# Chunk states summed by TensorE, the second group's units ahead of the weights, and low halves taken by a product with minus identity

## The chip, the cores and the metric

The kernel runs on one core of one Trainium2 chip. The metric is the device time of one execution in microseconds (us); the figure to beat is the median of several runs. Where a profile is shown, it is of one execution, and its engines are PE (TensorE matmuls), PEld (TensorE weight loads), DVE (VectorE), ACT (ScalarE), POOL (GpSimd) and SP (SyncE, which here only starts transfers).

## The reference

Two stages, in 32-bit floats. The first is gated linear attention with 4 batches, 8 heads, 768 positions and 48 values a head; the second is a feed-forward layer with GELU over all 3072 positions, 384 wide with 2048 hidden values. q, k, v and alpha come as 32-bit floats, the two weight matrices as 64-bit floats.

```python
for t in range(S):
    state = alpha[:, :, t, :, None] * state + einsum('bhd,bhe->bhde', k[:, :, t], v[:, :, t])
    y[:, :, t] = einsum('bhd,bhde->bhe', q[:, :, t], state)
x = y.transpose(0, 2, 1, 3).reshape(3072, 384)
h = x @ w_in
out = (0.5 * h * (1 + erf(h / sqrt(2)))) @ w_out
```

## The kernel before

**Attention.** The 3072 positions are 12 groups of 256 (three to a batch), and a group is handled in two units of four heads each, so there are 24 units. A unit's 256 positions are four chunks of 64. Running products of alpha along the positions, forward and backward, are DVE scans (`ahead`, lines 242 to 267); they scale q and k. On PE, `scores` (272) takes the products of k and q inside a chunk into a bank of PSUM, `turned` (285) transposes k there, ACT copies the transposed k out (`turned_out`, 294) and DVE masks the scores (`masked`, 299). `inside` (309) then writes one PSUM tile, `ybank`, that all units share: at line 319 the chunk's own part of the output, and at line 337 k times v for each chunk, which is what that chunk adds to the state. These are 64x64 products: the partitions hold chunk 0 or 2 in rows 0 to 63 and chunk 1 or 3 in rows 64 to 127, and two heads lie in the two halves of the output rows, so each product uses a quarter of the 128x128 array. A matmul with 32-bit floats shows as two PE instructions.

`chain` (346) adds these four contributions up on DVE, each onto the state before it, one instruction for each chunk (line 356, or a copy at 354 where a batch starts; the last chunk of a batch is left out). `outside_part` (369) multiplies q by the state ahead of its chunk into `ybank` (line 381), and waits for the last instruction of `chain`. `carry` (361) rescales the state for the next group.

**The split of x and of GELU.** The feed-forward products run in a shorter float format, fp32r, and each operand is kept as a high and a low half. ACT copies the finished `ybank` to the high half of x (`x_high`, 423); DVE subtracts that half from `ybank` to leave the low half (`x_low`, 427). `spread` (429) moves a strip of x between partitions by six transfers. For each group and each of eight slices f of 256 hidden values, `gemm1` (437) makes 18 matmuls (three products: high by high, low by high, high by low), ACT writes GELU twice (`gelus`, 455 and 456: rounded to the high half, and in full back into PSUM), DVE subtracts (`gelu_low`, 461) and `gemm2` (468) makes 12 matmuls into two accumulators that DVE empties when the group changes.

**The weights.** They arrive as 64-bit floats in 16 pieces, named a to p in turn from `w_in` and `w_out`; slice f needs pieces 2f and 2f+1. Each piece is turned into a high and a low half by ACT and DVE (`conversion`, 188): five DVE instructions, and a sixth at line 233 that leaves the low half. Three staging buffers hold pieces on the way.

**What sets the order.** The instruction order of PE, DVE, ACT and SP is written out ahead of time by a planner in the kernel (lines 585 to 821). It has a cost for each kind of step (`COST`), dependencies, and ranks; `ORDER` (31) gives the ranks of the first six units (digits) and of the pieces (letters). Each engine takes the ready step of lowest rank; PE fills the rest with `gemm1` and `gemm2`. The first three groups (`NSB`) run the feed-forward slices as pieces become ready; later groups follow when all pieces are converted. The order is then fixed: on the chip an engine waits at each instruction for what it needs. `pads` (99) fills unused rows of the operand tiles with 0 or 1 at the start.

Of the kernel before, what the change touches and what calls it, by code (L numbers as in the profile page):

```python
# [22 lines left out]
XB = 3  # L23
WAIT = 0.15
SLOW = 1.8
COST = dict(
    scan=2.25, back=2.05, q=1.35, scores=1.2, kn=0.6, mask=0.62, inside=1.2, chain=1.15, outer=0.85, carry=0.26,
    xh=0.6, xl=0.65, spread=2.0, check=0.95, load=2.6, fetch=0.4, u=0.92, c0=0.56, c1=0.9, c2=0.56, c3=0.95, c4=0.92,
    hi=0.84, lo=0.9, gemm1=2.12, gelu=0.58, low=0.63, gemm2=2.1, part=1.1,
)  # L30
ORDER = "0 1 a b c d 2 e 3 f g 4 h i 5 j k l m n o p"


@with_exitstack
def gla_then_gelu_ffn(ctx: ExitStack, tc: tile.TileContext, q, k, v, alpha, qg, kg, ag, w_in, w_out, out):
# [45 lines left out]
    def column(name, value):  # L81
        t = const.tile([P, 1], F32, name=name)
        nc.gpsimd.memset(t, value)
        return t

    zero, ones = column("zero", 0.0), column("ones", 1.0)
    lo_b, hi_b = column("lo_b", A_MIN), column("hi_b", -A_MAX)
    top = column("top", TOP).to_broadcast([P, G])
# [10 lines left out]
    def pads(i, n, p0, p1, eng):  # L99
        for r0 in (DP // 2, DP + DP // 2):  # L100
            r = slice(r0, r0 + DP // 2)
            t = data[i][n][r, p0:p1].rearrange("p a t -> p (a t)")
            if eng is nc.scalar:
                eng.copy(t, (ones if n == "a" else zero)[r].to_broadcast(t.shape))
            else:
                eng.memset(t, 1.0 if n == "a" else 0.0)

    for n in "akq":
        pads(0, n, 0, 1, nc.vector)
    for n, eng in (("a", nc.gpsimd), ("k", nc.scalar), ("q", nc.vector)):  # L110
        pads(0, n, 1, NPAIR, eng)
    for n, eng in (("a", nc.gpsimd), ("k", nc.scalar), ("q", nc.gpsimd)):
        pads(1, n, 0, NPAIR, eng)
    for t in vbuf:
        nc.gpsimd.memset(t[:, :, H * D :], 0.0)

    states = []
    for u in range(NU):
        states.append([const.tile([P, 2, D], F32, name=f"state{u}_{i}") for i in range(NCH + 1)])

    mask = const.tile([P, CS], F32, name="mask")
    nc.gpsimd.memset(mask, 1.0)
# [146 lines left out]
    def ends_batch(g, j):  # L269
        return g % GPB == GPB - 1 and j == NCH - 1  # L270
# [38 lines left out]
    def inside(g, u):  # L309
        d = cur[g, u]  # L310
        vn = vbuf[g % NB]
        for i in range(2):
            for j in range(NCH):
                c, b = j // 2, j % 2
                r, t = slice(b * CS, (b + 1) * CS), (2 * i + c) * CS
                for h in range(2):
                    o = slice(h * DP, (h + 1) * DP)
                    e = (4 * u + 2 * i + h) * D
                    nc.tensor.matmul(  # L319
                        ybank[o, b, t : t + CS],  # L320
                        lhsT=vn[r, c, e : e + DP],
                        rhs=d["ss"][r, h, 2 * i + c, :],
                        start=(i == 0 and c == 0),
                        stop=(j == 0 and g % GPB == 0),
                        skip_group_check=True,
                    )
        for j in range(NCH):
            if ends_batch(g, j):
                continue
            c, b = j // 2, j % 2  # L330
            r = slice(b * CS, (b + 1) * CS)
            for i in range(2):
                t = 2 * C + (2 * i + c) * D
                for h in range(2):
                    o = slice(h * DP, (h + 1) * DP)
                    e = (4 * u + 2 * i + h) * D
                    nc.tensor.matmul(  # L337
                        ybank[o, b, t : t + D],
                        lhsT=d["kn"][r, i, c * P + h * DP : c * P + (h + 1) * DP],
                        rhs=vn[r, c, e : e + D],  # L340
                        start=False,
                        stop=True,
                        skip_group_check=True,
                    )

    def chain(g, u):
        d = cur[g, u]
        st = states[u]
        for j in range(NCH):
            if ends_batch(g, j):  # L350
                continue
            new = ybank[:, j % 2, 2 * C : 2 * C + 4 * D].rearrange("p (i c d) -> p i c d", i=2, c=2)[:, :, j // 2]
            if g % GPB == 0 and j == 0:
                d["chain"] = nc.vector.tensor_copy(st[1], new)
            else:
                d["chain"] = nc.vector.tensor_tensor(out=st[j + 1], in0=new, in1=st[j], op=ALU.add)  # L356

    def carry(g, u):
        if ends_batch(g, NCH - 1):
# [65 lines left out]
    def x_low(g, u):  # L425
        for y, hi, lo in x_parts(g, u):
            nc.vector.tensor_tensor(out=lo, in0=y, in1=hi.bitcast(F32), op=ALU.subtract)

    def spread(g):
        x, z = cur[g, "x"], cur[g, "z"]  # L430
        for i in range(NK):
            for h in range(2):
                r0 = h * DP
                src = z[r0 + i * DR : r0 + (i + 1) * DR]
                eng = nc.scalar if h and g < NSB else nc.sync
                eng.dma_start(x[r0 + D : r0 + DP, i].bitcast(F32), src.bitcast(F32))

    def gemm1(g, f):
        xhi, xlo = xt[g]
        hp = ps_h.tile([P, 2, G], F32, tag="hp", name=f"hp_{g}_{f}")  # L440
        for j in range(2):
            for i in range(NK):
                for n, (a, x) in enumerate(((wi_hi[f], xhi), (wi_hi[f], xlo), (wi_lo[f], xhi))):
                    nc.tensor.matmul(  # L444
                        hp[:, j, :],
                        lhsT=a[:, j, i * P : (i + 1) * P],
                        rhs=x[:, i, :],
                        start=(i == 0 and n == 0),
                        stop=(i == NK - 1 and n == 2),
                    )  # L450
        return hp

# [6 lines left out]
    def gelu_low(g, f, hp, ghi):  # L459
        glo = ffn.tile([P, 2, G], F32R, tag="glo", name=f"glo_{g}_{f}")  # L460
        nc.vector.tensor_tensor(out=glo, in0=hp, in1=ghi.bitcast(F32), op=ALU.subtract)  # L461
        return glo

    parts = [const.tile([P, 2, DM], F32, name=f"part{i}") for i in range(NSB)]
    started = set()
# [144 lines left out]
    def op(*args, **kw):  # L610
        ops.append(Op(*args, **kw))
        return ops[-1]
# [4 lines left out]
    def plan_unit(n):  # L617
# [33 lines left out]
            free = [("x", g - XB - 1)]  # L651
        d["xh"] = op("ACT", "xh", lambda: (to_late(g, u), x_high(g, u)), [d["outer"]], rank=-1)
        d["free"] = free if u == 0 else []
        d["xl"] = op("DVE", "xl", lambda: x_low(g, u), [d["xh"]], rank=-0.5)
        if u == NU - 1:
            ready_x[g] = op("SP", "spread", lambda: spread(g), [d["xl"]], rank=-5, lands=2.2)
            if g >= NSB:
# [34 lines left out]
        return gemms.get((dep[1], NF2 - 1)) if next_f[dep[1]] == NF2 else False  # L692

    def when(o):
        d = next((v for v in unit.values() if v.get("xh") is o), None) if o.eng == "ACT" and o.cost == COST["xh"] else None
        at = o.at()
        if at is None or d is None:
            return at
        for dep in d["free"]:
            if isinstance(dep, tuple):  # L700
                dep = x_op(dep)
                if not dep:
                    return None
            if dep.end is None:
                return None
            at = max(at, dep.end + WAIT)
        return at
# [18 lines left out]
    def gemm1_op(g, t):  # L726
        f = next_f[g]
        next_f[g] += 1
        st = dict(g=g, f=f, first=g != state["g"], last=False)
        prev = steps[-1] if steps else None  # L730
        if st["first"]:
            if prev:
                prev["last"] = True
                prev["evac"] = Op("DVE", "part", lambda p=prev: p["out"](), [prev["gemm2"]], rank=-2)
                waiting["DVE"].append(prev["evac"])
            state["run"] += 1
        state["g"] = g
        two = steps[-2] if len(steps) > 1 else {}
        st["gemm1"] = Op("PE", "gemm1", lambda: st.update(hp=gemm1(g, f)))
        st["gelu"] = Op("ACT", "gelu", lambda: st.update(gh=gelus(g, f, st["hp"])), [st["gemm1"], two.get("gemm2")], rank=-3)  # L740
        st["gelu"].cost *= 2
        st["low"] = Op("DVE", "low", lambda: st.update(gl=gelu_low(g, f, st["hp"], st["gh"])), [st["gelu"], two.get("gemm2")], rank=-3)

        def second():
            if st["first"]:
                st["acc"] = [ps_o.tile([P, DM], F32, tag=f"acc{t}", name=f"acc{t}_{g}_{f}") for t in range(2)]
            else:
                st["acc"] = prev["acc"]
            st["out"] = gemm2(g, f, st["gh"], st["gl"], st["acc"], st["first"], st["last"], f == NF2 - 1)

        st["gemm2"] = Op("PE", "gemm2", second, [st["low"], prev and prev["gemm2"], prev and prev.get("evac")], rank=0)
        waiting["ACT"].append(st["gelu"])
        waiting["DVE"].append(st["low"])
        gemms[g, f] = st["gemm1"]
        steps.append(st)
        return st["gemm1"]
# [138 lines left out]
```

## Time and profile before

| | |
|---|---|
| median of 3 runs | 546.49 us (546.25 to 547.72) |
| the profiled execution | 546.99 us |
| its span, first to last instruction | 545.4 us |
| mean TensorE clock granted | 0.956 |
| PE busy | 508.4 us |
| DVE busy | 306.5 us |
| ACT busy | 201.3 us |
| POOL busy | 38.9 us |

Rows of groups give the line, the engine, the operation, what it writes and reads, the shape, the count, then busy time in us and the mean length of one in ns. Rows of time begin with the start in us from the span's start and the length in us. Lengths of matmuls overlap: the distance between starts is what one costs. In rows of stretches each engine's busy us and, in brackets, its instructions are given, then the clock that TensorE was granted as a share of full speed, the DMA share and GB/s.

### The profile page before, as it was taken

Reading aid. Unit: us, or ns where it says so; the run is one execution under the profiler, and the core shown is the slowest. Engines: PE = TensorE matmul, PEld = TensorE weight load, DVE = VectorE, ACT = ScalarE, POOL = GpSimd, SP = SyncE. Lnnn points to the kernel's source line nnn. Section 1 sums busy time; section 2 is a strip of 40 time slices with the busy share of each in tenths; the row PEclk is TensorE's granted clock in tenths of the full one; section 3 lists DMA queues with packets and bytes.
Section 4 is the critical chain, followed back from the end, with each engine's and each line's share of the span. In section 5 each row is a group of like instructions: output and inputs, shape, how many; then the busy total and the mean of one; then the engine's idle time right before and its main releaser. Section 6 shows DMA issues by size and latency. Waiting matters only on the chain.

```text
span 545.4 us, 13878 instructions
## 1 busy us (share of the span) xinstructions
PE 508.4 (93%) x5966; PEld 492.0 (90%) x5966; DVE 306.5 (56%) x573; ACT 201.3 (37%) x387; POOL 38.9 (7%) x51
## 2 busy tenths in 40 slices
PE   6547588999999999999999999999999999999996
PEld 6436588999999999999999999999999999999995
DVE  7999989999997878666337345142231221211211
ACT  3625345554443444433243243243223222222221
POOL 5000000000012121111001000000000000000000
PEclk9559589999999999999999999999999999999998
DMA  6974344533014344405005002001000000000001
GB/s 196 298 216 136 114 117 160 143 119 103 0 32 132 103 133 121 130 2 161 2 1 162 1 6 85 1 1 46 1 32 14 1 30 1 16 14 1 30 0 34
DMA packets 20723, 39.49 MB, mean 72 GB/s; under 512 B 4113, under 2 KB 7617, under 8 KB 20657
## 3 DMA queue, kind: packets, MB, share of 16 engines
q1 hardware_dynamic: 19136, 33.93, 20.7%
q0 software_dynamic: 1232, 4.33, 2.3%
q8 instruction: 49, 0.80, 0.6%
q10 hardware_dynamic: 288, 0.30, 0.2%
q14 instruction: 18, 0.14, 0.1%
HBM read 31.46 MB, written 4.72 MB: 66 GB/s over the span
## 4 chain that ended last, share of the span: by engine, by line
PE 84%; DVE 9%; DMA 2%; issue 2%; ACT 1%; ACTq 0%; DVEq 0%; SPq 0%
PE hp L444 37%; PE acc L472 35%; PE ybank L381 4%; PE s L290 2%; PE ybank L319 2%; PE s L281 2%; PE ybank L337 2%; DVE rp L262 1%; DVE st L217 1%; DVE pp L251 1%; DMA ad<-in_ag_dram 1%; DMA x<-z 1%; DVE w L202 1%; DVE state L356 1%; DVE w L227 1%
## 5 line engine op out<-in xcount | busy, mean ns | idle before, releaser
L444 PE MATMUL hp<-x,wih 128*128 128x256 f32 x1152 | 215.5, 287 | 7.6 <-DMA x<-z 7.6
L444 PEld LDWEIGHTS hp<-x,wih 128*128 128x128 f32 x1152 | 184.5, 193 | 8.9 <-ACT wih L230 7.8
L461 DVE TENSOR_TENSOR glo<-hp,ghi 128x512 fp32r<-128x512 f32 x96 | 66.1, 689 | 185.0 <-ACT hp L456 183.8
L444 PE MATMUL hp<-x,wil 128*128 128x256 f32 x576 | 163.9, 285 | 0.0
L455 ACT ACTIVATE ghi<-hp 128x512 fp32r<-128x512 f32 x96 | 57.5, 599 | 247.4 <-PE hp L444 247.3
L472 PE MATMUL acc<-woh,ghi 128*128 128x384 f32 x384 | 131.6, 343 | 1.4 <-ACT ghi L455 1.4
L472 PE MATMUL acc<-wol,ghi 128*128 128x384 f32 x384 | 128.6, 335 | 0.0
L444 PEld LDWEIGHTS hp<-x,wil 128*128 128x128 f32 x576 | 111.3, 193 | 0.0
L472 PE MATMUL acc<-woh,glo 128*128 128x384 f32 x384 | 82.2, 335 | 1.8 <-DVE glo L461 1.8
L472 PEld LDWEIGHTS acc<-woh,ghi 128*128 128x128 f32 x384 | 72.4, 188 | 2.6 <-ACT ghi L455 1.8
L472 PEld LDWEIGHTS acc<-wol,ghi 128*128 128x128 f32 x384 | 72.4, 189 | 0.0
L472 PEld LDWEIGHTS acc<-woh,glo 128*128 128x128 f32 x384 | 67.9, 188 | 2.2 <-DVE glo L461 2.2
L456 ACT ACTIVATE hp<-hp 128x512 f32<-128x512 f32 x96 | 57.1, 595 | 0.0
L258 POOL TENSOR_TENSOR qd<-qd,pp 128x512 f32<-128x512 f32 x18 | 23.2, 1287 | 226.0 <-DVE pe L252 158.3
L262 DVE TENSOR_TENSOR_SCAN rp<-ad,rp,top 128x255 f32<-128x255 f32 x48 | 35.3, 776 | 0.1
L381 PEld LDWEIGHTS ybank<-qd,state 48*48 48x48 f32 x704 | 23.7, 131 | 10.4 <-DVE state L356 6.6
L356 DVE TENSOR_TENSOR state<-ybank,state 128x96 f32<-128x96 f32 x80 | 20.5, 257 | 21.2 <-PE ybank L337 19.0
L381 PE MATMUL ybank<-qd,state 48*48 48x64 f32 x704 | 27.6, 233 | 5.3 <-DVE state L356 5.2
L251 DVE TENSOR_TENSOR_SCAN pp<-ad,top 128x256 f32<-128x256 f32 x48 | 30.4, 674 | 0.5 <-DMA ad<-in_ag_dram 0.5
L319 PEld LDWEIGHTS ybank<-ss,vn 64*64 64x64 f32 x768 | 14.5, 144 | 13.2 <-DVE ss L302 6.7
L319 PE MATMUL ybank<-ss,vn 64*64 64x64 f32 x768 | 18.0, 236 | 8.5 <-DVE ss L302 5.5
L496 POOL DMA_DIRECT2D out_dram<-part x11 | 8.3, 753 | 243.8 <-DVE part L490 164.6
(63 smaller groups left out, 397.0 us busy)
## 6 DMA issues: line engine op xcount, KB each, us to landing
st<-in_moe_w_in_dram SPq DMA_DIRECT2D x8, 768.0 KB, 4.8
st<-in_moe_w_out_dram SPq DMA_DIRECT2D x8, 768.0 KB, 4.8
ad<-in_ag_dram SPq DMA_DIRECT2D x48, 96.0 KB, 2.3
kd<-in_kg_dram SPq DMA_DIRECT2D x48, 96.0 KB, 2.3
qd<-in_qg_dram SPq DMA_DIRECT2D x48, 96.0 KB, 2.4
vn<-in_v_dram SPq DMA_DIRECT2D x12, 384.0 KB, 3.9
out_dram<-part POOLq DMA_DIRECT2D x11, 384.0 KB, 3.7
x<-z SPq DMA_DIRECT2D x63, 32.0 KB, 2.9
```

The source lines that it names most:

```text
L251: nc.vector.tensor_tensor_scan(pp[:, i], at[:, i], top, MID, ALU.mult, ALU.min)
L258: nc.gpsimd.tensor_tensor(out=qt, in0=qt, in1=pp, op=ALU.mult)
L262: nc.vector.tensor_tensor_scan(rp[:, i, G - 2 :: -1], at[:, i, G - 1 : 0 : -1], top[:, 1:], rp[:, i, G - 1 :], ALU.mult, ALU.min)
L281: nc.tensor.matmul(d["s"][o, h, e : e + CS], lhsT=d["kt"][r, i, t], rhs=d["qt"][r, i, t], start=True, stop=True)
L319: nc.tensor.matmul(ybank[o, b, t : t + CS], lhsT=vn[r, c, e : e + DP], rhs=d["ss"][r, h, 2 * i + c, :], start=(i == 0 and c == 0), stop=(j ...
L356: d["chain"] = nc.vector.tensor_tensor(out=st[j + 1], in0=new, in1=st[j], op=ALU.add)
L381: ins = nc.tensor.matmul(ybank[r, b, t : t + CS], lhsT=states[u][j][r, i], rhs=d["qt"][r, i, j * CS : (j + 1) * CS], start=False, stop=Tru ...
L444: nc.tensor.matmul(hp[:, j, :], lhsT=a[:, j, i * P : (i + 1) * P], rhs=x[:, i, :], start=(i == 0 and n == 0), stop=(i == NK - 1 and n == 2),)
L455: nc.scalar.activation(ghi, hp, AF.Gelu)
L456: nc.scalar.activation(hp, hp, AF.Gelu)
L461: nc.vector.tensor_tensor(out=glo, in0=hp, in1=ghi.bitcast(F32), op=ALU.subtract)
L472: nc.tensor.matmul(acc[t], lhsT=a[:, j, t * C : (t + 1) * C], rhs=w[:, j, :], start=(first and j == 0 and k == 0 and w is wo_hi[f]), stop= ...
```

## The change

Six edits.

1. **State sums in PSUM.** `inside` no longer writes each chunk's own contribution but the sum of all contributions up to and with the chunk: for chunks 2 and 3 the products of the first 128 positions and of the next are both accumulated. Where both chunks of a half are wanted, one product takes all 128 rows. `chain` is then one DVE instruction for a unit, which adds the carried state to all four sums (or copies them). The last chunk of a batch is no longer left out.
2. **Order.** The units of group 1 (2 and 3) go ahead of all weight pieces, and units 4 and 5 between pieces f and g.
3. **Low half of x, in the first three groups.** PE multiplies the high half by minus identity and accumulates into `ybank` (`x_minus`); ACT copies what is left (`x_rest`). DVE's subtraction goes.
4. **Low half of GELU, in the first three groups while the planner's clock is under 80 us.** The same: one matmul of 512 columns into the PSUM tile, and a copy by ACT (`gelu_rest`).
5. **One start flag for a tile in `gemm1`,** so that the later matmul accumulates on both halves.
6. **Pads.** DVE fills the pads of the first two pairs for all three tensors; the rest of q's goes to ACT. A minus identity is made by DVE at the start.

```diff
-    hi=0.84, lo=0.9, gemm1=2.12, gelu=0.58, low=0.63, gemm2=2.1, part=1.1,
+    hi=0.84, lo=0.9, gemm1=2.12, gelu=0.58, minus=0.35, low=0.63, gemm2=2.1, part=1.1,
-ORDER = "0 1 a b c d 2 e 3 f g 4 h i 5 j k l m n o p"
+ORDER = "0 1 2 3 a b c d e f 4 5 g h i j k l m n o p"
...
+    minus = const.tile([P, P], F32R, name="minus")
+    nc.vector.tensor_scalar(out=minus, in0=ident, scalar1=-1.0, scalar2=None, op0=ALU.mult)
...
     for n in "akq":
-        pads(0, n, 0, 1, nc.vector)
-    for n, eng in (("a", nc.gpsimd), ("k", nc.scalar), ("q", nc.vector)):
-        pads(0, n, 1, NPAIR, eng)
+        pads(0, n, 0, 2, nc.vector)
+    for n, eng in (("a", nc.gpsimd), ("k", nc.scalar), ("q", nc.scalar)):
+        pads(0, n, 2, NPAIR, eng)
...
         for j in range(NCH):
-            if ends_batch(g, j):
-                continue
-            c, b = j // 2, j % 2
-            r = slice(b * CS, (b + 1) * CS)
+            b = j % 2
             for i in range(2):
-                t = 2 * C + (2 * i + c) * D
+                t = 2 * C + (2 * (j // 2) + i) * D
                 for h in range(2):
                     o = slice(h * DP, (h + 1) * DP)
                     e = (4 * u + 2 * i + h) * D
-                    nc.tensor.matmul(
-                        ybank[o, b, t : t + D],
-                        lhsT=d["kn"][r, i, c * P + h * DP : c * P + (h + 1) * DP],
-                        rhs=vn[r, c, e : e + D],
...
+                    for c in range(j // 2 + 1):
+                        r = slice(0, P if c < j // 2 or b else CS)
+                        nc.tensor.matmul(
+                            ybank[o, b, t : t + D],
+                            lhsT=d["kn"][r, i, c * P + h * DP : c * P + (h + 1) * DP],
+                            rhs=vn[r, c, e : e + D],
...
     def chain(g, u):
         d = cur[g, u]
...
+        new = ybank[:, :, 2 * C : 2 * C + 4 * D].rearrange("p b (c e) -> p b c e", c=2)
+        to = held[u][:, 1:].rearrange("p (c b) e -> p b c e", b=2)
+        if g % GPB == 0:
+            d["chain"] = nc.vector.tensor_copy(to, new)
+        else:
+            old = held[u][:, 0].unsqueeze(1).unsqueeze(1).to_broadcast([P, 2, 2, 2 * D])
+            d["chain"] = nc.vector.tensor_tensor(out=to, in0=new, in1=old, op=ALU.add)
...
+    def x_minus(g, u):
+        for y, hi, _ in x_parts(g, u):
+            for b in range(2):
+                nc.tensor.matmul(
+                    y[:, :, :, b], lhsT=minus, rhs=hi[:, :, :, b], start=False, stop=True, skip_group_check=True
+                )
+
+    def x_rest(g, u):
+        for y, _, lo in x_parts(g, u):
+            nc.scalar.copy(lo, y)
...
+    def gelu_rest(g, f, hp, ghi):
+        nc.tensor.matmul(hp, lhsT=minus, rhs=ghi, start=False, stop=True, skip_group_check=True)
+
+        def out():
+            glo = ffn.tile([P, 2, G], F32R, tag="glo", name=f"glo_{g}_{f}")
+            nc.scalar.copy(glo, hp)
+            return glo
+
+        return out
...
-        d["xl"] = op("DVE", "xl", lambda: x_low(g, u), [d["xh"]], rank=-0.5)
+        if g < NSB:
+            d["xm"] = op("PE", "minus", lambda: x_minus(g, u), [d["xh"]], rank=-1)
+            d["xl"] = op("ACT", "xh", lambda: x_rest(g, u), [d["xm"]], rank=-1)
+        else:
+            d["xl"] = op("DVE", "xl", lambda: x_low(g, u), [d["xh"]], rank=-0.5)
...
+        if g < NSB and t < UNTIL:
+            st["minus"] = Op("PE", "minus", lambda: st.update(rest=gelu_rest(g, f, st["hp"], st["gh"])), [st["gelu"]], rank=-3)
+            st["low"] = Op("ACT", "gelu", lambda: st.update(gl=st["rest"]()), [st["minus"], two.get("gemm2")], rank=-2.9)
+            waiting["PE"].append(st["minus"])
```

In the planner `UNTIL` is 80.0 and the cost of `chain` goes from 1.15 to 0.5; that of `inside` stays at 1.2.

More of the change, by code (lines that the diff above doesn't have):

```diff
@@ L25 @@
 SLOW = 1.8
+UNTIL = 80.0
 COST = dict(
-    scan=2.25, back=2.05, q=1.35, scores=1.2, kn=0.6, mask=0.62, inside=1.2, chain=1.15, outer=0.85, carry=0.26,
+    scan=2.25, back=2.05, q=1.35, scores=1.2, kn=0.6, mask=0.62, inside=1.2, chain=0.5, outer=0.85, carry=0.26,
     xh=0.6, xl=0.65, spread=2.0, check=0.95, load=2.6, fetch=0.4, u=0.92, c0=0.56, c1=0.9, c2=0.56, c3=0.95, c4=0.92,
-    hi=0.84, lo=0.9, gemm1=2.12, gelu=0.58, low=0.63, gemm2=2.1, part=1.1,
+    hi=0.84, lo=0.9, gemm1=2.12, gelu=0.58, minus=0.35, low=0.63, gemm2=2.1, part=1.1,
 )
-ORDER = "0 1 a b c d 2 e 3 f g 4 h i 5 j k l m n o p"
+ORDER = "0 1 2 3 a b c d e f 4 5 g h i j k l m n o p"
 @with_exitstack
@@ L115, in gla_then_gelu_ffn @@
         nc.gpsimd.memset(t[:, :, H * D :], 0.0)
-    states = []
-    for u in range(NU):
-        states.append([const.tile([P, 2, D], F32, name=f"state{u}_{i}") for i in range(NCH + 1)])
+    held = [const.tile([P, NCH + 1, 2 * D], F32, name=f"state{u}") for u in range(NU)]
+    states = [[t[:, j].rearrange("p (i d) -> p i d", i=2) for j in range(NCH + 1)] for t in held]
     mask = const.tile([P, CS], F32, name="mask")
@@ L336, in inside @@
                     e = (4 * u + 2 * i + h) * D
-                    nc.tensor.matmul(
-                        ybank[o, b, t : t + D],
-                        lhsT=d["kn"][r, i, c * P + h * DP : c * P + (h + 1) * DP],
-                        rhs=vn[r, c, e : e + D],
[L341 to L344, printed above, removed]
+                    for c in range(j // 2 + 1):
[4 more added lines that the diff above has]
+                            rhs=vn[r, c, e : e + D],
+                            start=False,
+                            stop=True,
+                            skip_group_check=True,
+                        )
     def chain(g, u):
         d = cur[g, u]
[L348 to L356, printed above, removed]
+        new = ybank[:, :, 2 * C : 2 * C + 4 * D].rearrange("p b (c e) -> p b c e", c=2)
[5 more added lines that the diff above has]
+            d["chain"] = nc.vector.tensor_tensor(out=to, in0=new, in1=old, op=ALU.add)
     def carry(g, u):
@@ L427, in x_low @@
             nc.vector.tensor_tensor(out=lo, in0=y, in1=hi.bitcast(F32), op=ALU.subtract)
+    def x_minus(g, u):
[3 more added lines that the diff above has]
+                    y[:, :, :, b], lhsT=minus, rhs=hi[:, :, :, b], start=False, stop=True, skip_group_check=True
+                )
+    def x_rest(g, u):
+        for y, _, lo in x_parts(g, u):
+            nc.scalar.copy(lo, y)
     def spread(g):
@@ L447, in gemm1 @@
                         rhs=x[:, i, :],
-                        start=(i == 0 and n == 0),
+                        start=(j == 0 and i == 0 and n == 0),
                         stop=(i == NK - 1 and n == 2),
+                        skip_group_check=True,
                     )
@@ L694, in when @@
     def when(o):
-        d = next((v for v in unit.values() if v.get("xh") is o), None) if o.eng == "ACT" and o.cost == COST["xh"] else None
+        d = next((v for v in unit.values() if v.get("xh") is o), None) if o.name == "xh" else None
         at = o.at()
@@ L752, in gemm1_op @@
         waiting["ACT"].append(st["gelu"])
-        waiting["DVE"].append(st["low"])
+        waiting[st["low"].eng].append(st["low"])
         gemms[g, f] = st["gemm1"]
```

## The prediction

> **What bounds the kernel now.** I read the page first: the span and the slices.
>
> ```profile
> span 545.4 us, 13878 instructions
> ...
> PE   6547588999999999999999999999999999999996
> ```
>
> A digit is PE's busy share, in tenths, of a slice of 13.6 us. PE is full from the eighth slice to the end. So there are two stages, an opening of about 100 us and a long rest. The stretches give what each engine does in them.
>
> ```profile
> 50.00:100.00 50.00, 39.19 (x537) 35.62 (x536) 47.29 (x84) 22.98 (x43) 0.00 (x0) 0.83 0.41 128
> 54.10:71.20 17.10, 11.60 (x181) 10.59 (x182) 16.23 (x30) 5.00 (x10) 0.00 (x0) 0.50 0.44 123
> 100.00:400.00 300.00, 300.00 (x3932) 290.44 (x3931) 186.66 (x366) 119.19 (x243) 28.56 (x25) 1.00 0.23 68
> ```
>
> In the second half of the opening DVE is busy 47.29 us of 50 and PE 39.19: PE has gaps while DVE has next to none. From 100 us PE has no gap, at the full clock: what is added to PE there is added to the end, what is taken from DVE there is worth nothing. Between 50 and 100 us PE loses 50 - 39.19 = 10.8 us idle, and 11.60 us of work at half clock (54.1 to 71.2) would have taken half, another 5.8 us. That is 16.6 us. Before 50 us PE has gaps too, but until the first weights and the first x there is little to fill them with. So the change is a trade: less on DVE in the opening, against more on PE everywhere.
>
> **Part 1, the state sums: what PE pays.** The change removes three of four DVE adds and adds matmuls at line 337. Before, a unit has 4 chunks x 2 x 2 = 16 products, 32 PE instructions. After, chunks 2 and 3 have two products each, so 24 products, 48 instructions, and at the end of a batch, where there were 12, also 24. The shape changes too: 16 of the 24 use all 128 rows. What does one cost?
>
> ```profile
> 207.92 0.86 PE L472 MATMUL acc<-woh,glo 128*128 128x384 f32 x4
> 208.71 0.82 PE L381 MATMUL ybank<-qd,state 48*48 48x64 f32 x22
> 209.33 0.27 PE L281 MATMUL s<-qd,kd 48*64 48x64 f32 x2
> 209.36 0.23 PE L381 MATMUL ybank<-qd,state 48*48 48x64 f32 x2
> ...
> 213.18 0.68 PE L337 MATMUL ybank<-vn,kn 64*64 64x48 f32 x32
> 213.79 0.50 PE L444 MATMUL hp<-x,wih 128*128 128x256 f32 x2
> 214.13 0.28 PE L444 MATMUL hp<-x,wil 128*128 128x256 f32 x1
> 214.25 0.28 PE L444 MATMUL hp<-x,wih 128*128 128x256 f32 x1
> ```
>
> ```profile
> L337 PE MATMUL ybank<-vn,kn x704: 205/218/338, 16.7 to 402.9; 64*64 64x48 f32 x176
> ```
>
> One instruction of line 337 lasts 0.218 us, so the starts of the 32 spread over 0.68 - 0.22 = 0.46 us. They lie in four quarters of the array (two halves of rows, two of columns), so a quarter takes 8 of them in 0.46 us: 0.058 us each. Line 381 uses two quarters only: 22 instructions, 11 in each, over 0.82 - 0.22 = 0.60 us, that is 0.060 us over ten steps. So a quarter needs about 0.058 us for an instruction whether two or four quarters work, and they work on their own: line 281 begins in a free quarter at 209.33, ahead of the last of line 381 at 209.36.
>
> A product of 128 rows takes both row halves of its column half. Each column half has 12 products, 24 instructions, and all of them use the upper row half: 24 x 0.058 = 1.39 us in place of 0.46. That is 0.93 us more for a unit, and at the end of a batch, where there were six steps, 18 more instead of 16. No row shows a product of 128 rows by 64 columns, so the price is bounded from both sides. Below: line 444 moves 256 columns in 0.12 us (214.13 to 214.25), so 48 columns moved twice need 0.045 us by its rate, and the unit 24 x 0.045 = 1.08 us. Above: if PE must empty before it goes from one shape of product to another. That shows at the seams: four of line 472 at 0.17 us from 207.92 would have let line 381 begin at 208.61, it begins at 208.71; the last of line 337 begins at 213.64, and 0.058 later is 213.70, line 444 begins at 213.79 and its first two take 0.34 in place of 0.24. So a change of shape costs 0.10 to 0.19 us. In chunk 2 the change alternates between 128 and 64 rows: with the two changes around it that would be nine seams in a unit. I take 0.058 without seams, since it rests on rows of the same shape in columns and the quarters run independently.
>
> The TensorEngine Tiling (Array Packing) page of the Trainium skill, under Tiling Modes, Key Properties, says otherwise: "Changing tiling mode (not just tile) drains the TensorE", and it lists 128x64 and 64x64 as different configurations. By it the seams would be paid, and the sum would be that of the second rival. The trace agrees for 128x128 against quarters (the 0.10 to 0.19 us); it holds no case of the pair in question.
>
> In the full stage lie groups 3 to 11, 18 units, six at the end of a batch. Steps after: 18 x 24 = 432. Before: 12 x 8 + 6 x 6 = 132. Added: 300 x 0.058 = **+17.4 us**, with nothing to hide it.
>
> **Part 2, what DVE gains.**
>
> The groups of DVE, then one of ACT:
>
> ```profile
> L262 DVE TENSOR_TENSOR_SCAN rp<-ad,rp,top 128x255 f32<-128x255 f32 x48 | 35.3, 776 | 0.1
> L251 DVE TENSOR_TENSOR_SCAN pp<-ad,top 128x256 f32<-128x256 f32 x48 | 30.4, 674 | 0.5 <-DMA ad<-in_ag_dram 0.5
> L356 DVE TENSOR_TENSOR state<-ybank,state 128x96 f32<-128x96 f32 x80 | 20.5, 257 | 21.2 <-PE ybank L337 19.0
> ...
> L202 DVE SCALAR_TENSOR_TENSOR w<-st,u 128x768 int32<-128x768 int32 x16 | 15.3, 957 | 0.4
> ...
> L490 DVE COPY part<-acc 128x384 f32<-128x384 f32 x23 | 11.7, 550 | 2.5 <-PE acc L472 2.5
> L212 DVE TENSOR_SCALAR u<-w 128x768 int32<-128x768 int32 x16 | 8.9, 556 | 0.3
> ...
> L427 DVE TENSOR_TENSOR x<-ybank,x 128x512 fp32r<-128x512 f32 x12 | 8.2, 682 | 0.0
> ```
>
> ```profile
> L423 ACT CAST x<-ybank 128x512 fp32r<-128x512 f32 x12 | 7.1, 588 | 9.5 <-PE ybank L381 9.5
> ```
>
> For a unit: `chain` goes from four at 0.26 (1.03) to one of the size of the accumulator copy, 0.55; the subtraction for x, 0.68 or a little more in two parts, goes. That is 1.2 us for each of six units, 7 us. GELU's subtraction, of the shape of line 427's, goes at 0.68 for about six steps under the planner's 80 us, 4 us. So DVE has some 11 us less to do in the opening. ACT gets as many copies, 0.59 each, about 7 us on an engine that is busy for 23 of the 50 us to 100: hidden, unless a copy that waits for PE holds up the conversions queued behind it on ACT (their results feed DVE); I estimate under 2 us, in the range.
>
> PE pays too. A low half of x is 512 columns through minus identity, two times 0.12 by line 444, plus a change of shape, say 0.4 us a unit. A GELU step is 512 columns, 0.24 us.
>
> **Part 3, the order.** The first scan, and then the last step of the second piece of the first, third and fifth slice of the eight, which says when these weights are ready now:
>
> ```profile
> 5.53 1.27 DVE L251 TENSOR_TENSOR_SCAN pp<-ad,top 128x256 f32<-128x256 f32 x2 [0.52 <-DMA ad<-in_ag_dram]
> ...
> 27.69 0.95 DVE L233 TENSOR_TENSOR wol<-w,woh 128x768 fp32r<-128x768 f32 x1
> ...
> 65.48 0.95 DVE L233 TENSOR_TENSOR wol<-w,woh 128x768 fp32r<-128x768 f32 x1
> ...
> 102.99 0.95 DVE L233 TENSOR_TENSOR wol<-w,woh 128x768 fp32r<-128x768 f32 x1
> ```
>
> A unit costs DVE about 7.1 us now: two scans each way (2.9), two scalings and the mask of 128x512 at 0.68 (2.0), chain (1.0), low half (0.7) and small ones; after, 5.9. A piece has four instructions like line 202 and two like line 212, 4.9 us, so a slice 9.9. After, four units come first: the first scan at about 5.5 (it waits for its transfer) plus 4 x 5.9 is 29, then slices at about 39, 49 and 59, units 4 and 5 until 71, slices at 81 and 91. The first slice is 10 us later, the third 7 earlier, the fifth 13 earlier. The loads of units 2 and 3 are moved on SP's queue ahead of three fetches of weights; DVE has 29 us of units to do meanwhile, so a first piece that lands some 5 us later is still in time.
>
> What PE can do with it hangs on x. All units share `ybank`, so each must be finished before the next writes it.
>
> ```profile
> 15.80 1.13 PE L319 MATMUL ybank<-ss,vn 64*64 64x64 f32 x32 [4.14 <-DVE ss L302]
> 16.71 1.10 PE L337 MATMUL ybank<-vn,kn 64*64 64x48 f32 x32
> ...
> 24.33 1.13 PE L319 MATMUL ybank<-ss,vn 64*64 64x64 f32 x32 [2.92 <-DVE x L427]
> ...
> 36.94 0.77 PE L444 MATMUL hp<-x,wih 128*128 128x256 f32 x2 [7.59 <-DMA x<-z]
> ```
>
> The period is 24.33 - 15.80 = 8.5 us now. After, line 337 takes 16 more steps of about 0.1 at half clock (1.10 - 0.30 over eight), +1.7; the shorter chain gives back 0.5; a matmul and a copy in place of a subtraction add 0.6: about 10 us. Unit 0 at 15, so unit 3 ends near 55, its copies with it, and with the transfer x of group 1 arrives near 59 (now 7.59 us pass from the last product of unit 1 to the first `gemm1`, copies and transfer together). The first `gemm1` stays near 37 to 39 (x now, weights after). At 50 us PE stands about where it does now: one slice of group 0 through, half a step less of the second, one unit's share more. From 59 on there is work for two groups: three slices each, 17 us, with units 4 and 5 some 10 us more, then slices at 81 and 91 for three groups. So PE should be full from about 59 us, in place of about 95. Of the 16.6 us lost now after 50 us I leave 7: half of 50 to 59 with its slow clock, and some gaps at the units. **Gain 10 us.** Bounds: 0 if group 1 comes as late as before, 21 if nothing is lost after 50 us and unit 3's PE work (about 4.5 us) is done by then.
>
> PE's added work in the opening that is not hidden, after 59 us: two and a half units at 0.93 and two more batch-end steps each in units 4 and 5 (2.6), the low halves of x for three units (1.0), five GELU products (1.2): **+4.8 us**. Minus identity, pads and start flag: the memsets move between engines by 0.2 to 0.5 us ahead of a first scan that waits for its transfer; nothing.
>
> **The sum,** against the profiled execution's 546.99 us (545.4 plus 1.6 around it): + 17.4 - 10 + 4.8 = 559.2; the median lies 0.5 lower, so **558.7 us**.
>
> **The rivals.** *Cheap products, faster.* If a product of 128 rows costs only its stream, 0.045 us, the full stage gains 432 x 0.045 - 132 x 0.058 = 11.8 us and the opening 3.7; with the opening's gain between 10 and 21 us that is 541 to 552, and faster from a gain of 15.5 us on. For it: `ybank` is finished sooner as well. Against it: 48 and 64 columns cost the same 0.058 to 0.060 in the rows, so the stream isn't what sets it. 0.22. *Seams.* If each change of shape inside line 337 empties PE: nine times 0.10 to 0.19, and chunk 2's sixteen instructions run one after another in place of in pairs (+0.46), so 1.4 to 2.2 us a unit over 20.5 units, 28 to 45 us: 587 to 603, about 595. For it: the seams that the rows show. Against it: no row shows one between products with equal columns. 0.20. *No gain in the opening.* PE's longer units at half clock hold `ybank`, group 1's x comes as late as now, and the gain is 0: 568.7. 0.10. That edit 4 does little because few steps fall under the planner's 80 us would move the sum by 1 us and is in the range.
>
> **How the numbers follow.** The forecast has 0.48, with its own range 549 to 568. About 0.3%, or 1.6 us, is what a measurement can tell from no change. Faster: 0.13 from the cheap products and 0.02 from the forecast's edge, 0.15. Same: 0.04 and 0.03, 0.07. Slower: the rest, 0.78. The range leaves out the best 0.08 of the cheap products and half of the seams, about 0.11: 543 to 594.
>
> **What would show it.** Line 337: 1152 instructions instead of 704, and in the full stage 1.4 us from its first start to the next line's (1.1 with cheap products, 3 with seams). Line 356 gone, one instruction of 128x384 near 0.55. PE without gaps from about 60 us, the half-clock stretch of 54 to 71 us gone. The slices of PE full at the end as before. I am wrong if line 337 costs under 1 us a unit, or if PE is full well before 50 us.

## The result

The changed kernel takes 595.73 us (593.87 to 597.41) against 546.85: 8.9% more, ratio 1.0892 (1.0855 to 1.0928). The range of the prediction ended at 594. The direction, and that TensorE pays for the state sums, came as forecast; the size is that of the second rival, the seams.

The page after, in part: the shares of the engines, the slices of PE, the chain that ended last, and the groups of the state sums on PE and DVE.

```profile
span 594.4 us, 14762 instructions
...
PE 576.1 (97%) x6437; PEld 548.3 (92%) x6437; DVE 298.7 (50%) x494; ACT 206.6 (35%) x403; POOL 38.5 (6%) x51
...
PE   6998998999999999999999999999999999999996
...
PE hp L454 35%; PE acc L493 34%; PE ybank L338 13%; PE ybank L380 4%; PE ybank L321 3%; PE s L292 2%; PE s L283 2%; DVE rp L264 0%; ACT hp L467 0%; PE hp L476 0%; ACTq L446 0%; DVE pp L253 0%; ACT ghi L466 0%; ACT x L437 0%; PE ybank L431 0%
...
L338 PE MATMUL ybank<-vn,kn 128*64 128x48 f32 (+1 forms) x1152 | 82.6, 239 | 0.0
...
L355 DVE TENSOR_TENSOR state<-ybank,state 128x384 f32<-128x384 f32 x16 | 8.9, 557 | 54.4 <-PE ybank L338 54.4
```

PE was 508.4 us busy, now 576.1. The state sums (line 338 now, 337 before) were 2% of the chain and are 13%. DVE's `chain` is one instruction of 0.557 us, as forecast, and waits 54.4 us for those products.

A unit of the full stage after, and then one at the end of a batch before (the prediction shows a usual one before, at 213.18):

```profile
100.23 0.69 PE L321 MATMUL ybank<-ss,vn 64*64 64x64 f32 x32
100.75 3.20 PE L338 MATMUL ybank<-vn,kn 64*64 64x48 f32 x48
103.88 0.39 PE L454 MATMUL hp<-x,wih 128*128 128x256 f32 x1
```

```profile
97.97 0.62 PE L337 MATMUL ybank<-vn,kn 64*64 64x48 f32 x24
98.52 0.45 PE L472 MATMUL acc<-woh,ghi 128*128 128x384 f32 x1
```

From the first start of the sums to the next line's start: 103.88 - 100.75 = 3.13 us, where 1.39 was forecast and 0.61 (0.55 at the end of a batch) stood before. All 18 units of the full stage take 3.13: 18 x 3.13 - 12 x 0.61 - 6 x 0.55 = 45.7 us of the 48.9 measured. The other 3.2 us, uncertain by some 2 us as the interval of the ratio is, were lost in the opening. Inside the unit, in stretches cut at chunks 0, 1, 2 and 3, with the instructions of this line alone (those still running from the stretch before are counted again):

```profile
100.74:101.05 0.31, 0.30 (x8) 0.27 (x8) 1.00 0.00 0
101.05:101.33 0.28, 0.28 (x12) 0.27 (x9) 1.00 0.00 0
101.33:103.24 1.91, 1.91 (x22) 1.48 (x18) 1.00 0.19 26
103.24:103.88 0.64, 0.64 (x18) 0.58 (x16) 1.00 0.61 115
```

Chunks 2 and 3 have 16 instructions each. Chunk 3's are all of 128 rows and take 0.64 us with the way out to the next line; chunk 2's alternate between 128 and 64 rows and take 1.91, that is 0.24 for each of eight products.

The second half of the opening and the full stage, in the same stretches as before:

```profile
50.00:100.00 50.00, 45.98 (x621) 41.57 (x620) 43.02 (x64) 26.62 (x52) 1.29 (x1) 0.96 0.50 155
100.00:400.00 300.00, 300.00 (x3705) 284.72 (x3704) 177.36 (x296) 106.80 (x215) 26.37 (x23) 1.00 0.22 64
```

Between 50 and 100 us PE is busy 45.98 us (39.19 before), at a granted clock of 0.96 (0.83), and the half-clock stretch of 54 to 71 us is gone. That is not a gain yet, since the longer sums count as busy. The first half of the opening, before and then after:

```profile
0.00:50.00 50.00, 29.23 (x443) 26.86 (x444) 44.28 (x78) 23.06 (x36) 7.48 (x22) 0.73 0.69 210
0.00:50.00 50.00, 41.28 (x523) 36.47 (x524) 38.45 (x70) 22.27 (x40) 7.21 (x22) 0.63 0.63 190
```

Here the clock is lower than it was, 0.63 in place of 0.73, and at half clock the first unit's sums take 5.04 us to the next line's start where 0.83 stood before. The first `gemm1` begins late, at 48.01 in place of 36.94:

```profile
48.01 0.79 PE L454 MATMUL hp<-x,wih 128*128 128x256 f32 x2
```

What the feed-forward layer had done by 100 us, `gemm1` and `gemm2` before, then the same two after (busy us and count of PE, then of PEld):

```profile
0.00:100.00 100.00, 19.36 (x126) 18.60 (x126) 0.78 0.55 169
0.00:100.00 100.00, 15.93 (x80) 13.73 (x81) 0.78 0.55 169
...
0.00:100.00 100.00, 15.28 (x107) 14.53 (x108) 0.80 0.56 173
0.00:100.00 100.00, 12.86 (x60) 11.95 (x60) 0.80 0.56 173
```

The changed kernel is behind by 19 and 20 matmuls, with the sums of six units done in both. So the opening, which was to gain, lost a little. From 100 us PE is as busy as it was, 300 us of 300, with fewer instructions in them, 3705 for 3932: the waits inside the sums show as busy time.

### The profile page after: what moved, and what is told of

It reads as the page before. It is cut to its first block, busy times and chain, and to the rows that moved or that the text cites. A ratio compares the mean times of both kernels' runs of the same rounds, so it can differ in the third digit from the quotient of the medians.

```text
span 594.4 us, 14762 instructions
## 1 busy us (share of the span) xinstructions
PE 576.1 (97%) x6437; PEld 548.3 (92%) x6437; DVE 298.7 (50%) x494; ACT 206.6 (35%) x403; POOL 38.5 (6%) x51
## 4 chain that ended last, share of the span: by engine, by line
PE 94%; DVE 3%; ACT 1%; issue 1%; ACTq 0%; DVEq 0%
PE hp L454 35%; PE acc L493 34%; PE ybank L338 13%; PE ybank L380 4%; PE ybank L321 3%; PE s L292 2%; PE s L283 2%; DVE rp L264 0%; ACT hp L467 0%; PE hp L476 0%; ACTq L446 0%; DVE pp L253 0%; ACT ghi L466 0%; ACT x L437 0%; PE ybank L431 0%
## 5 line engine op out<-in xcount | busy, mean ns | idle before, releaser
L454 PE MATMUL hp<-x,wih 128*128 128x256 f32 x1152 | 213.3, 285 | 0.0
L472 DVE TENSOR_TENSOR glo<-hp,ghi 128x512 fp32r<-128x512 f32 x91 | 62.7, 689 | 184.7 <-ACT hp L467 184.6
L338 PE MATMUL ybank<-vn,kn 128*64 128x48 f32 (+1 forms) x1152 | 82.6, 239 | 0.0
L338 PEld LDWEIGHTS ybank<-vn,kn 128*64 128x64 f32 (+1 forms) x1152 | 68.3, 145 | 12.7
L299 ACT COPY kn<-s 128x512 f32<-128x512 f32 x24 | 14.1, 587 | 86.7 <-PE ybank L338 72.3
L264 DVE TENSOR_TENSOR_SCAN rp<-ad,rp,top 128x255 f32<-128x255 f32 x48 | 36.6, 803 | 0.1
L355 DVE TENSOR_TENSOR state<-ybank,state 128x384 f32<-128x384 f32 x16 | 8.9, 557 | 54.4 <-PE ybank L338 54.4
```

The source lines that it names most:

```text
L264: nc.vector.tensor_tensor_scan(rp[:, i, G - 2 :: -1], at[:, i, G - 1 : 0 : -1], top[:, 1:], rp[:, i, G - 1 :], ALU.mult, ALU.min)
L299: nc.scalar.copy(d["kn"], d["s"][:, :, 2 * C : 4 * C])
L338: nc.tensor.matmul(ybank[o, b, t : t + D], lhsT=d["kn"][r, i, c * P + h * DP : c * P + (h + 1) * DP], rhs=vn[r, c, e : e + D], start=False ...
L454: nc.tensor.matmul(hp[:, j, :], lhsT=a[:, j, i * P : (i + 1) * P], rhs=x[:, i, :], start=(j == 0 and i == 0 and n == 0), stop=(i == NK - 1 ...
```

## The experiments

The ratios are to the kernel before as timed beside each run (medians of 547.60 to 547.68 us).

**1. The same products, grouped by shape** (e1_grouped).

```diff
-        for j in range(NCH):
+        for j, c in ((0, 0), (2, 1), (1, 0), (2, 0), (3, 0), (3, 1)):
...
-                    for c in range(j // 2 + 1):
```

> The changed kernel with the same 24 products of the state sums in another order: first the eight of 64 rows, then the sixteen of 128 rows, so that nine changes of shape in a unit become one. Theory (each change of shape empties TensorE, 0.15 us): a unit's sums take 8 x 0.058 + 0.15 + 16 x 0.058 = 1.54 us in place of 3.13, 18 full-stage units give back 28.6 us, the opening a few more: 559 to 567. Rival (the products themselves or their number are dear, 48 instructions at 0.065 us): nothing changes, 594 to 597. Second rival (two products in a row that add to the same place in PSUM wait for each other): also about 563, since chunk 2's pairs are taken apart too; the next run tells it from the theory.

**2. The same order, chunk 2 all of 128 rows** (e2_rows128).

```diff
-                        r = slice(0, P if c < j // 2 or b else CS)
+                        r = slice(0, P if j else CS)
```

> The changed kernel in its own order, but chunk 2's second product takes 128 rows like its neighbours, so that chunk 3 is wrongly counted in chunk 2's sum: the same count, order and places in PSUM, only eight of nine changes of shape gone. Theory (change of shape): 0.23 + 0.15 + 20 x 0.058 = 1.54 us a unit, 559 to 567 in all. Rival (two products in a row into the same place wait): 3.1 us a unit, 594 to 597. Rival (number of products): 594 to 597.

**3. Five changes of shape in place of nine** (e8_five_seams): the alternating order for one `i` of chunk 2, and for the other both products of 64 rows first, then both of 128.

```diff
...
+        todo += [(2, 0, h, c) for h in range(2) for c in range(2)]
+        todo += [(2, 1, h, c) for c in (1, 0) for h in range(2)]
...
```

> The changed kernel with chunk 2's products taken apart by shape for one of two pairs of heads only: five changes of shape in a unit in place of nine, and half of the products that had to run alone. Theory: 28 x 0.058 + 5 x 0.15 = 2.37 us a unit, between 3.13 and 1.62, and 577 to 581 in all. Rival (one change of shape in the unit is enough to lose all, or only the last ones count): near 595 or near 562.

A unit of the full stage in each, in that order:

```profile
168.89 1.69 PE L337 MATMUL ybank<-vn,kn 64*64 64x48 f32 x48
170.51 0.39 PE L453 MATMUL hp<-x,wih 128*128 128x256 f32 x1
```

```profile
174.47 1.72 PE L338 MATMUL ybank<-vn,kn 64*64 64x48 f32 x48
176.12 0.39 PE L454 MATMUL hp<-x,wih 128*128 128x256 f32 x1
```

```profile
164.94 2.46 PE L340 MATMUL ybank<-vn,kn 64*64 64x48 f32 x48
167.33 0.44 PE L495 MATMUL acc<-woh,ghi 128*128 128x384 f32 x1
```

| kernel | changes of shape | a unit's sums, us | median, us | ratio to before |
|---|---|---|---|---|
| changed | 9 | 3.13 | 595.73 | 1.0892 (1.0855 to 1.0928) |
| five seams | 5 | 2.39 | 579.14 | 1.0577 (1.0538 to 1.0616) |
| rows 128 | 1 | 1.65 | 562.97 | 1.0278 (1.0231 to 1.0326) |
| grouped | 1 | 1.62 | 561.51 | 1.0271 (1.0229 to 1.0314) |

All have 48 instructions a unit. The number of products is not the cause, since it never changes. Two products in a row that add to the same place are not the cause either: experiment 2 keeps them at 1.65 us a unit, and chunk 3 of the changed kernel has them too. What changes is the shape, and the price follows the count: from one to five, 2.39 - 1.62 = 0.77 us, of which four products that run alone in place of in pairs take 4 x 0.058 = 0.23; the rest is 0.135 us for each change. From five to nine it is much the same: 0.74 less 0.23 is 0.51, 0.128 for each. The starts inside a unit of the changed kernel agree: the first instruction after a change starts 0.15 us after the one ahead of it, in place of 0.058, and its partner 0.094 after that, together 0.128 more. What TensorE does in that time no run shows; the profile models the ends of matmuls, so it can't show the array empty.

**4. The sums alone, and all but the sums** (e4_sums_only, e3_no_sums: the edits to `inside`, `chain` and the state tiles put into the kernel before, or taken out of the changed one, with the planner's cost of `chain`).

> The kernel before with the state sums alone. Theory: 46 us in the full stage and some 2.5 to 4 us for each of the last opening units: 595 to 605, about 599. Rival (the new order and the copies on ScalarE are a good part of the loss): 570 to 590.

> The changed kernel with the state sums undone: the chunks' own contributions and four adds on VectorE, as before; the order, the products with minus identity and the pads stay. Theory: the whole loss is the sums' (18 x 2.52 + 6 x 0.15 = 46 us in the full stage, and 2 to 20 us of the opening), and the other edits help: 528 to 541, about 535. Rival (the new order costs too, since the first weights come 19 us later): 547 to 552.

The sums alone: 601.24 us, ratio 1.0972 (1.0954 to 1.0990). All but the sums: 540.93, ratio 0.9876 (0.9854 to 0.9898), at the upper end of what was expected. So the sums are the whole loss, and the rest is a gain of 6.7 us; 53.6 lost and 6.7 gained leave 46.9, which is the measured 48.9 within the noise.

**5. Where the opening's gain comes from** (e6_order_only, the edit shown on the kernel before; e7_old_order, the run without the sums with this line as it was before).

```diff
-ORDER = "0 1 a b c d 2 e 3 f g 4 h i 5 j k l m n o p"
+ORDER = "0 1 2 3 a b c d e f 4 5 g h i j k l m n o p"
```

> The kernel before with the new order alone: group 1's units ahead of the weights, sums and low halves on VectorE as before. Theory (half of the opening's gain is that both groups share each slice): 542 to 546. Rival (only the relief of VectorE helps, and the later weights cost): 547 to 552.

> The run without the state sums, in the old order: the products with minus identity and the pads alone. Theory (half the gain is the relief of VectorE, some 8 us of subtractions): 542 to 545. Rival (the relief is worth its full length): 538 to 541; rival (copies on ScalarE and waits of TensorE eat it up): 546 to 549.

The order alone takes 548.88, ratio 1.0027 (1.0005 to 1.0048): a miss, no gain. The products with minus identity and the pads in the old order take 544.28, ratio 0.9932 (0.9909 to 0.9956), as expected. One reason why the order alone is worth nothing shows on ScalarE. The run with the order alone:

```profile
11.67 0.58 ACT L297 COPY kn<-s 128x512 f32<-128x512 f32 x1 [5.63 <-PE s L290]
...
22.00 0.89 ACT L194 ACTIVATE u<-st 128x768 f32<-128x768 f32 x1 [8.91 <-DMA st<-in_moe_w_in_dram]
...
23.50 0.57 ACT L297 COPY kn<-s 128x512 f32<-128x512 f32 x1
```

ScalarE stands 8.91 us before the scaling of the first weight piece, whose transfer now comes after those of units 2 and 3, and unit 1's copy of k is queued behind it until 23.50. In the run without the sums VectorE stands 4.0 us (3.89 with the order alone) before the mask that waits for that copy:

```profile
24.00 0.69 DVE L305 TENSOR_TENSOR ss<-s,mask 128x512 f32<-128x512 f32 x1 [4.03 <-ACT kn L300]
```

**6. That copy ahead of the scaling** (e5_copy_first on the run without the sums, e9_order_copy_first on the order alone).

```diff
         plan_unit(n)
+    wops[0]["u"].deps.append(unit[1]["kn"])
```

> The run without the state sums, with one dependency more in the planner: on ScalarE the copy of unit 1's transposed k goes ahead of the scaling of the first weight piece, which waits until 21.9 us for its transfer and holds that copy from about 18.7 to 23.4. Theory (the moved weight transfers hold up ScalarE, and behind it the units): unit 1 comes 4 us earlier, the idle 4.0 us of VectorE at 20 to 24 us goes, and 2 to 4 us of it reach the end: 537 to 539. Rival (the opening is bound by the weights on VectorE alone): no change, 540 to 542.

> The kernel before with the new order and, on ScalarE, unit 1's copy of the transposed k ahead of the scaling of the first weight piece. Theory (the new order itself helps, and the wait for the piece's transfer took that back): the 4 us at 20 to 24 us go and 544 to 546 is left, against 548.9 with the order alone. Rival (the order is worth nothing without the relief of VectorE): 547.5 to 550.

In the first of the two, ScalarE and then VectorE:

```profile
18.78 0.59 ACT L300 COPY kn<-s 128x512 f32<-128x512 f32 x1 [4.99 <-PE s L293]
22.01 0.92 ACT L197 ACTIVATE u<-st 128x768 f32<-128x768 f32 x1 [2.64 <-DMA st<-in_moe_w_in_dram]
```

```profile
19.93 0.68 DVE L305 TENSOR_TENSOR ss<-s,mask 128x512 f32<-128x512 f32 x1
```

The mask runs at 19.93 in place of 24.00. The median goes from 540.93 to 537.26, ratio to before 0.9825 (0.9796 to 0.9855); with the order alone from 548.88 to 545.94, ratio 0.9968 (0.9950 to 0.9985). Both as expected: about 3 to 4 us of the 4 reach the end. 537.26 us is the lowest median measured here, below both kernels.

**7. GELU's products, and another order,** on the run of 537.26 us (e10_no_gelu_product: `UNTIL = 0.0`; e11_mixed_order).

```diff
-ORDER = "0 1 2 3 a b c d e f 4 5 g h i j k l m n o p"
+ORDER = "0 1 2 a b 3 c d e f 4 g h 5 i j k l m n o p"
```

> The run without the sums and with the copy first, but with all low halves of GELU on VectorE again (none of the five products). Theory (five subtractions of 0.69 us off a full VectorE): 1 to 4 us slower, 538 to 541. Rival (the waits for TensorE and ScalarE eat it up): no change, 536.5 to 538.

> The run without the sums and with the copy first, in an order between the two: units 0 to 2, pieces a and b, unit 3, pieces c to f, unit 4, g and h, unit 5, the rest. Theory (VectorE is full either way; the first slice comes some 5 us earlier, group 1's x some 10 later): 535 to 541. Rival (group 1 ahead of all weights is what counts): 541 to 544.

Without the GELU products 540.73, ratio 0.9865 (0.9835 to 0.9895): about 3.5 us more by the medians, as much as five subtractions at 0.69. The runs overlap a little (539.09 to 543.04 against 536.55 to 540.23), so the size is rough. In the mixed order 538.26, ratio 0.9815 (0.9786 to 0.9843): almost the interval of the run that it changes, so no need shows for group 1 to come ahead of all weights.

## Why the prediction was wrong

**The step that failed** is the choice in part 1: "I take 0.058 without seams, since it rests on rows of the same shape in columns and the quarters run independently." The quarters do run independently of each other, and a product of 128 rows does cost 0.058 us in its column half, two halves side by side: grouped by shape, a unit takes 1.62 us where 1.39 and one seam of 0.135 would make 1.53 (the rest is the way out: the next line starts 0.15 us after the last start, 0.09 more than inside a shape, and that step was in the 0.61 of before too). But a change between 64 and 128 rows costs time, as one between a quarter and the whole array does. The prediction counted nine seams and priced the case right, 587 to 603, gave it 0.20, and ended its range at 594, under that rival's middle of 595. The rows bore it out further than I weighed them. Both changes that the prediction measured cost 0.10 to 0.19 us. The full stage of before has 79 passages between the whole array and its quarters, and at each the next start comes about 0.09 us later than inside a shape; only products that differ in size but all lie in quarters (48 or 64 rows and columns, lines 381 and 281) follow one another without a price. That the pair of shapes was not among them was no reason to set it at nothing. The rule of the Trainium skill (TensorEngine Tiling (Array Packing), Tiling Modes, Key Properties) is that a change of tiling mode drains the engine. The runs agree with it in that each such change has a price, here about 0.13 us; the draining itself they do not show.

**Where the miss lies.** Between the forecast and the time are 37.0 us. Of these 28.3 lie in the full stage (45.7 against 17.4), and about 8.4 in the opening, which lost 3.2 where a net gain of 5.2 was forecast.

**The sum without that step.** With one seam in place of nine the run takes 561.51 us; the forecast without seams was 558.7. So the other terms were about right together: the count of 300 steps, the opening's gain less PE's added work there. From the grouped run it is 18 x 1.62 - 10.6 = 18.6 us in the full stage against 13.9 us in all, so the opening gave 4.7 net, give or take 2. Within that noise the failed step accounts for both parts of the miss.

**The parts of the opening** were not as written, so that their sum came out has luck in it. DVE's relief was right in size (0.557 for `chain`; five GELU steps, not six). In the last order the GELU steps are worth about their length, 3.5 us; in the old order the products with minus identity and the pads together give 3.3 us, for some 7.5 us taken off DVE (six units at 0.68, five steps at 0.69). The order was forecast to carry the gain; alone it carries 0.3% the other way, and a step of part 3 failed: "DVE has 29 us of units to do meanwhile, so a first piece that lands some 5 us later is still in time." VectorE had work, but the piece is first scaled on ScalarE, where it held a unit's copy; and it landed 8 us later (the scaling, which waited for it both times, began at 13.58 before and at 21.46 after). The prediction looked for a hold-up on ScalarE the other way round, a copy that holds up the conversions. Nor did the first `gemm1` stay near 37 to 39: it began at 48.01, at 44.6 without the sums, and at 41.2 with the copy ahead as well. Without the hold-up the order gives 1.7 us alone; the other edits without it give 3.3; together 10.3. That they help each other fits the two stages of the opening (x for two groups early, and weights early), but which wait is saved by both is argued and not shown.

**The rivals.** "Cheap products" is out: 0.058 holds at 48 columns. "No gain in the opening" has the time wrong, but its mechanism is not out: in the changed kernel the longer units at half clock came with a late first `gemm1` and an opening that lost 3.2 us. With the sums grouped the opening gave 4.7 us, and without the sums the kernel takes 540.93.

## What to carry to other kernels

Count the changes between products of 64 and of 128 rows on TensorE as work of their own, here about 0.13 us each: the same 24 products cost 3.13 or 1.62 us by their order alone. Work taken from a full VectorE and given to TensorE paid here only where TensorE had gaps; 18 of 24 units lay where it had none, and there PE stayed 300 us of 300 busy while it got less done. When transfers are moved, look at the first instruction that reads them on each engine, and at what is queued behind it.

## What the runs showed of the hardware

In the grouped run, products of 128 rows by 64 columns run in pairs in the two column halves at 0.058 us an instruction with 48 columns to move, the same as products of 64 by 64 (line 381 has 0.060 with 64 columns to move). A change between the two shapes costs 0.128 to 0.135 us at the full clock. Adding twice in a row to the same place in PSUM costs at most the 0.03 us a unit between experiments 2 and 1 (1.65 and 1.62 us).
